# New due times for a list scheduler, and the last output tile stored in two halves

## The chip, the cores and the metric

The kernel runs on one core of one Trainium2 chip. The metric is the device time of one execution in microseconds. Three runs of the kernel before the change took 478.75, 477.60 and 477.36 us, a median of 477.6 us. One further execution was profiled: it took 473.72 us, of which the profile's span covers 472.0 us.

## What is computed

The reference is a transformer layer on 2048 tokens of 576 features: a layer norm, a segmented attention with a running memory, a residual, a second layer norm, a two-layer network with GELU, and a second residual. Cut to what matters:

```
x: [1, 2048, 576]; 32 heads of 18; 4 segments of 512 tokens; F = 4608
q, k, v = layernorm(x) @ wq, @ wk, @ wv
for each segment s:
    p     = softmax(q_s k_s^T * scale + causal mask)
    a_dot = p @ v_s
    a_mem = phi(q_s) M / (phi(q_s) z + 1e-6)       # M, z: sums over earlier segments
    o_s   = g * a_mem + (1 - g) * a_dot            # g = sigmoid(beta), one a head
    M, z += phi(k_s)^T v_s, sum of phi(k_s)
h   = x + o @ wo
out = h + gelu(layernorm(h) @ w1 + b1) @ w2 + b2
```

## The kernel before the change

The tokens are cut into 8 chunks of 256 (index c), each of two token tiles of 128 rows (index tl or qt). In this document tile t is tile 2c + tl, so tiles 0 to 15. Everything that is multiplied is bf16, and sums are f32 in PSUM.

The kernel is not written in the order in which it runs. It holds generators ("streams"), one for each kind of work, and a small planner that interleaves them while the program is being built:

- stream_P (two of them, one a tile of each chunk): load x, layer norm (lines 420 to 440), transpose to xT, the q, k, v products (lines 417 and 418, right operand wqkv), eviction by ScalarE or VectorE (lines 497 and 498), transposes of q and k to QT and KT, and phi(k).
- stream_M: the running memory (line 576) and its copies.
- stream_A: attention in visits of 16 score products (line 618), one exp over 128x2048 on ScalarE (line 624), a causal mask on GpSimd or VectorE (lines 629 and 631), 16 products with v (line 650, called PV here), the memory products (line 673), and then `finish`, which divides and adds up into o_nat (VectorE lines 686 to 694, GpSimd line 695).
- stream_B (one a tile): transpose o_nat to xT, the product with wo (lines 417 and 418, right operand wo_t), add x, layer norm, transpose to xn2T, add b2 and store the result h to a scratch tensor hd in DRAM.
- stream_F1: the products with w1 (tails of 64 rows on line 912, main part on line 925; the first chunk on lines 885 and 887), bias on eviction (VectorE 935, ScalarE 933), GELU on ScalarE (line 947). The weights w1 are loaded again for every chunk, 512 columns at a time, by one large DMA (line 838, 512 KB) and two small ones (line 841, 32 KB each). This trio is called a w1 group here.
- stream_F2: the products with w2 (line 974, 36 for each half of 288 columns), add h (line 978, from hc, which line 963 reloads from hd), store the tile (line 981).

From chunk 2 on, transposes of x (xT<-xn) and of q and k are done by DMA, from chunk 1 on those of o (xT<-o_nat) and of the second norm (xn2T). All these, and all loads and stores but one, are issued by SyncE through line 189 and its sisters. **SyncE issues in program order**: an issue that waits for its data holds back every issue behind it.

The planner (`step`, at the end of the kernel) walks a clock of its own. Each operation has a planned duration, its data dependencies, and a due time `now + slack`. When an engine is free in the planner's clock, the ready operation with the earliest due time is issued next:

```
for o in queue[e]:
    if o.ready() <= now and (best is None or (o.due, o.made) < (best.due, best.made)):
        best = o
```

The slacks are a table of some 45 numbers, `SLACK`, one a kind of operation (`t_o` the transposes of o_nat, `w1` the weight groups, `mask` the causal masks, `sum` the GpSimd sum into o_nat, and so on). Three more, `lead`, `balance` and `alone` with `linger`, choose which stream TensorE takes next. `PHASES` is a list of (time, changes): when the planner's clock passes a time, the table is updated. Before the change it has 8 entries after the initial table: at 30, 40, 100, 130, 160, 220, 320 and 360 us. The chip knows nothing of these times. All that is left of them on the chip is **the fixed order of the instructions on each engine**.

Of the kernel before, what the change touches and what calls it, by code (L numbers as in the profile page):

```python
# [16 lines left out]
def kernel(  # L17
# [15 lines left out]
    nc = tc.nc  # L33
    P = 128
    x = A_x.flatten_outer_dims()
    of = out.flatten_outer_dims()
# [4 lines left out]
    NCH = S // Q  # L41
# [17 lines left out]
    def sbuf(name, shape, dt=BF16):  # L59
        return sb.tile([P] + shape, dt, name=name)  # L60
# [9 lines left out]
    SLACK = dict(zero=19, head=36, lnp=38.5, lnb=53, pow=-202, apply=-44.5, ek_k=497.5, relu_k=102, min_k=61, add_k=34.5,  # L70
                 mz=152.5, exp=-105.5, ek=-79.5, relu=-88.5, min=192.5, add=160, hb=-200.5, gelu=56, finish=35.5, mem=-80,
                 sum=23.5, out=-77.5, hd=122.5, xp=-148, xb=-22.5, t_x=-121.5, t_q=365, t_k=36, t_o=175.5, t_h=161, w1=101,
                 w2=116.5, hc=-15, evict=-236.5, qk=-22.5, ot=126.5, mask=78.5, lead=42.5, balance=254, alone=0, linger=1.5,
                 g=9.5, x1=80, hold=-133.5, ln0=-100)
    PHASES = [(30, dict(zero=31.5, head=69.5, lnp=42, pow=-174, apply=-18.5, ek_k=572, relu_k=123, min_k=-8, add_k=97, mz=106.5,
                        exp=-54.5, ek=-116, relu=-108, min=107, add=93.5, hb=-324.5, gelu=23, mem=-91.5, sum=101, out=-68.5, hd=157,
                        xp=-263, xb=-6, t_x=-129, t_q=354.5, t_k=103, t_o=169.5, t_h=165, w1=131.5, w2=55, hc=105.5, evict=-327.5,
                        qk=-50.5, ot=42.5, mask=66, lead=41.5, balance=124, g=87.5, x1=50.5, hold=-192.5, ln0=34.5)),
              (40, dict(zero=42.5, head=90.5, lnp=70.5, lnb=54, pow=-230, apply=-8.5, ek_k=562, relu_k=120, min_k=-17.5, add_k=55.5,
                        mz=109, exp=-26.5, ek=-166.5, relu=-81, min=99.5, add=85.5, gelu=18.5, finish=19.5, mem=-67.5, sum=115,  # L80
                        out=-75.5, hd=194, xp=-259, xb=-60, t_x=-133, t_k=49.5, t_o=146, t_h=205, w1=129.5, w2=-3.5, hc=124.5,
                        evict=-359.5, qk=-86, ot=26, mask=65, lead=42.75, balance=118, linger=1, g=88.5, x1=47, hold=-202.5,
                        ln0=85.5)),
              (100, dict(zero=10.5, head=94.5, lnp=22.5, lnb=46, apply=-5.5, relu_k=153, min_k=-12.5, mz=117, exp=21.5, ek=-169,
                        min=99, add=89.5, hb=-307, gelu=26, sum=115.5, out=-60.5, xp=-288.5, xb=-55.5, t_x=-114, t_q=353.5,
                        t_k=48.5, t_o=131, t_h=216.5, w1=130, w2=-19.5, hc=124, evict=-323.5, qk=-104, ot=30, mask=53, lead=41.75,
                        balance=117.5, g=86.5, x1=31, hold=-200.5)),
              (130, dict(lnp=38, lnb=63.5, relu_k=119, min_k=-28, add_k=105, mz=66.5, min=116, add=113.5, gelu=21, finish=17,
                        mem=-95.5, sum=133, t_x=-113, t_q=352, t_o=170, w1=123.5, w2=83.5, evict=-359.5, mask=70, lead=42.25,
                        x1=66.5, hold=-184.5, ln0=35)),  # L90
              (160, dict(zero=-30, head=52, lnp=36.5, lnb=80, pow=-237, apply=-37.5, ek_k=649, relu_k=225, min_k=3, add_k=42.5,
                        mz=36, exp=-28.5, ek=0, relu=-118.5, min=95.5, add=61.5, hb=-372.5, gelu=16, finish=12.5, mem=-133.5,
                        sum=123, out=-107.5, hd=219, xp=-333.5, xb=-93, t_x=-80.5, t_q=338, t_k=89.5, t_o=196, t_h=205.5, w1=124.5,
                        w2=101, hc=197.5, evict=-388.5, qk=-68.5, ot=23.5, mask=34.5, lead=37.75, balance=116, linger=2.5, g=112,
                        x1=55.5, hold=-120.5, ln0=-55)),
              (220, dict(head=-75, lnp=4.5, lnb=77, pow=-250, apply=-3, ek_k=675, relu_k=249.5, min_k=-6, add_k=138, mz=-68, exp=-38,
                        ek=2, relu=-158, min=129.5, add=53, hb=-380, gelu=10.5, finish=-7, mem=-85, sum=125, out=-97.5, hd=166.5,
                        xp=-354.5, xb=-44, t_x=-87, t_q=371.5, t_k=169, t_o=155, t_h=225.5, w1=139, w2=105.5, hc=214.5,
                        evict=-346.5, qk=-100.5, ot=31, lead=43, balance=141, linger=1, g=138.5, x1=56.5, hold=-173, ln0=-88.5)),
              (320, dict(zero=-28, head=-73, lnb=77.5, apply=-2, relu_k=281.5, add_k=136, mz=-68.5, relu=-142, hb=-396, finish=-7.5,  # L100
                        hd=174.5, xp=-350.5, xb=-45.5, t_x=-47, t_q=371, t_k=169.5, qk=-84, ot=27, mask=74.5, alone=0.3, x1=89.5,
                        ln0=-89)),
              (360, dict(zero=-34, lnp=5.5, lnb=93.5, pow=-238, ek_k=659, relu_k=282.5, min_k=-9, mz=-118.5, exp=-35, ek=17,
                        relu=-158, min=121.5, add=51, hb=-392, finish=24.5, sum=142.5, out=-96.5, hd=167.5, xp=-354.5, xb=-6,
                        t_q=355, t_k=153.5, t_o=154, t_h=181, w1=139.5, w2=109.5, hc=233.5, evict=-376.5, qk=-83, ot=26.5,
                        mask=73.5, lead=44.75, balance=135, alone=0.6, linger=0.3, g=170, x1=75.5, hold=-175))]
    ops = []
    now, dma_free, table, tiling = 0.0, 0.0, "exp", 128
    SWITCH = 0.092
# [8 lines left out]
    class Op:  # L118
        start, end, at, apart, two, hold, ways = None, NEVER, None, False, False, 0.0, None
# [42 lines left out]
    def op(eng, dur, issue, rd=(), wr=(), slack=0.0, table=None, port=None, n=2, mode=128):  # L162
        o = Op(eng, dur, issue, preds_of(rd, wr), now + slack, table)
        o.n, o.mode = n, mode
        o.port = eng == "POOL" if port is None else port
        ops.append(o)
        queue[eng].append(o)
        note(o, rd, wr)
        return o
# [7 lines left out]
    def transfer(o, kb, first, rd, wr, receipt=0.0):  # L177
        d = Op("DMA", kb, None, (), 0.0)
        d.first, d.receipt = first, receipt
        o.moves = d  # L180
        note(d, rd, wr)
        return d

    def dma(kb, issue, rd=(), wr=(), slack=0.0):
        return transfer(op("SP", 0.5, issue, rd, wr, slack), kb, 1.6, rd, wr, {288: 0.1, 144: 0.7, 576: 0.8, 72: 0.6, 864: 1.4}.get(kb, 1.0))
# [114 lines left out]
    ek = sbuf("ek", [H, Dh])  # L300
# [6 lines left out]
    hc = sbuf("hc", [HALF], F32)  # L307
    ot = sbuf("ot", [D])
# [3 lines left out]
    hd = tc.dram_tile([S, D], F32, name="hd")  # L312
# [99 lines left out]
    def mm(n):  # L412
        return n * MM + 0.003
# [541 lines left out]
    def stream_F2():  # L955
        for c in range(NCH):
            hT = hTs[c % 2]
            for tl in range(2):
                t = 2 * c + tl
                for hf in range(2):  # L960
                    hs = slice(hf * HALF, (hf + 1) * HALF)
                    yield need(lambda: c in gelued, bank_slots, [("hT", c % 2, 0)])
                    dma(144, lambda t=t, hs=hs: nc.sync.dma_start(out=hc[:], in_=hd[t * P:(t + 1) * P, hs]), [("hd", t)], ["hc"], SLACK["hc"])
                    b = bank_slots.take()
                    for f in range(0, NF, 4):
                        hk = [("hT", c % 2, f // 2), ("hT", c % 2, f // 2 + 1)]
                        if f:
                            yield need(None, None, hk)
                        work["F2"] += 0.5

                        def go(f=f, b=b, hT=hT, tl=tl, hs=hs):
                            acc = banks[b][:, 0:HALF]
                            for q in range(f, f + 4):
                                nc.tensor.matmul(out=acc, lhsT=hT[:, q, tl * P:(tl + 1) * P], rhs=w2_sb[:, q, hs],  # L974
                                                 start=(q == 0), stop=(q == NF - 1))

                        op("PE", 4 * mm(HALF), go, hk + [("w2", f // 6), ("w2", (f + 3) // 6)], [b], n=8)
                    op("DVE", 0.45, lambda b=b, hs=hs: nc.vector.tensor_tensor(out=ot[:, hs], in0=banks[b][:, 0:HALF], in1=hc[:], op=ALU.add),
                       [b, "hc"], [("ot", hf)], slack=SLACK["ot"])
                    bank_slots.give(b)  # L980
                dma(144, lambda t=t: nc.sync.dma_start(out=of[t * P:(t + 1) * P, :], in_=ot[:]), [("ot", 0), ("ot", 1)], (), SLACK["out"])
            done_F2.add(c)

    F1, F2 = stream_F1(), stream_F2()
# [107 lines left out]
```

## Time and profile before

| what | value |
|---|---|
| median of three runs | 477.6 us (477.36 to 478.75) |
| the profiled execution, and its span | 473.72 us, 472.0 us |
| TensorE (PE) busy | 462.4 us, 98% of the span, 6102 matmuls |
| ScalarE (ACT) busy | 337.7 us, 72% |
| VectorE (DVE) busy | 272.8 us, 58% |
| GpSimd (POOL) busy | 182.6 us, 39% |
| DMA | 80.9 MB, mean 171 GB/s |
| first matmul starts, last matmul ends | 1.24 us, 468.85 us |
| granted TensorE clock | 1.0 throughout |

An engine's share is taken over the whole span. TensorE is the engine that is busy nearly all the time, so a microsecond saved on another engine shows in the time only where TensorE would have waited for it. A matmul counts as busy until its result is out, which is later than the moment at which the next one can start. The distance from one matmul's start to the next one's is therefore the better measure of what a product costs: 122 ns for 288 columns, 109 ns for 256, 182 ns for 432, 25 ns for a PV product.

### The profile page before, as it was taken

What the parts mean: (1) busy time and instruction counts of PE and PEld (TensorE: products, weight loads), DVE (VectorE), ACT (ScalarE), POOL (GpSimd) and SP (SyncE); (2) the same over time, 40 slices, a digit from 0 to 9 for tenths busy, and PEclk for the clock granted to TensorE, in tenths of its full rate; (3) what the DMA queues carried; (4) which work ended last, traced back from release to release, by engine and by line L of the source; (5) the groups of instructions that cost most, each with busy time, mean ns of one, the idle gap of its engine ahead of it and who ended that gap; (6) DMA issues with size and microseconds to landing.
All of it is one profiled execution on the core that took longest, in us unless ns stands there. A gap on an engine that the chain in (4) does not pass through costs nothing.

```text
span 472.0 us, 14508 instructions
## 1 busy us (share of the span) xinstructions
PE 462.4 (98%) x6102; PEld 350.5 (74%) x6102; DVE 272.8 (58%) x695; ACT 337.7 (72%) x331; POOL 182.6 (39%) x242
## 2 busy tenths in 40 slices
PE   8999999998999999999999999999999999999997
PEld 6768777675677777666687777677777788888875
DVE  4899975997765444788764438767545341111101
ACT  6787769966898868877678687877869787355400
POOL 4666451794734323778452306557224010000000
PEclk9999999999999999999999999999999999999999
DMA  8997878577986555979766658879565478543011
GB/s 231 269 304 236 162 159 257 105 159 153 162 231 183 143 152 171 192 146 199 111 139 195 179 168 214 149 208 232 171 184 166 132 207 238 181 134 108 26 50 50
DMA packets 123009, 80.90 MB, mean 171 GB/s; under 512 B 57520, under 2 KB 120896, under 8 KB 122944
## 3 DMA queue, kind: packets, MB, share of 16 engines
q1 hardware_dynamic: 122912, 79.98, 66.5%
q8 instruction: 47, 0.77, 0.7%
q14 instruction: 18, 0.15, 0.1%
q0 software_dynamic: 32, 0.01, 0.0%
HBM read 60.03 MB, written 7.08 MB: 142 GB/s over the span
## 4 chain that ended last, share of the span: by engine, by line
PE 82%; DMA 8%; DVE 4%; POOL 2%; ACT 1%; issue 1%; SPq 0%; POOLq 0%; ACTq 0%
PE bank L974 20%; PE bank L925 18%; PE bank L417 10%; PE late L974 7%; PE ox L650 6%; DMA xT<-o_nat 4%; PE st L618 4%; PE late L925 3%; PE bank L912 3%; PE bank L418 2%; PE bank L885 2%; DMA wqkv<-in_A_wk_dram 2%; PE ox L925 1%; POOL pt L629 1%; ACT pt L624 1%; PE ox L974 1%
## 5 line engine op out<-in xcount | busy, mean ns | idle before, releaser
L624 ACT ACTIVATE pt<-st 128x2048 bf16<-128x2048 f32 x80 | 150.2, 1877 | 43.5 <-PE st L618 40.0
L974 PEld LDWEIGHTS <-hT 128*128 128x128 bf16 x1152 | 110.2, 98 | 28.2 <-ACT hT L947 0.2
L974 PE MATMUL bank<-w_sb,hT 128*128 128x288 bf16 x864 | 121.3, 286 | 0.0
L629 POOL TENSOR_SCALAR_AFFINE_SELECT pt<-pt 128x512 bf16<-128x512 bf16 x86 | 57.2, 677 | 109.1 <-ACT pt L624 104.3
L925 PE MATMUL bank<-xn2T,w1g 128*128 128x256 bf16 x688 | 84.4, 273 | 0.0
L935 DVE TENSOR_TENSOR hT<-bank,b1T 128x512 bf16<-128x512 f32 x67 | 46.2, 690 | 59.7 <-PE bank L925 59.3
L925 PEld LDWEIGHTS <-w1g 128*128 128x128 bf16 x752 | 69.3, 97 | 12.2 <-issue 3.8
L947 ACT ACTIVATE hT<-hT 128x1536 bf16<-128x1536 bf16 (+3 forms) x24 | 66.3, 2763 | 0.5
L417 PE MATMUL bank<-wqkv,xT 128*128 128x432 bf16 (+1 forms) x268 | 57.2, 336 | 0.6 <-DMA wqkv<-in_A_wk_dram 0.6
L417 PEld LDWEIGHTS <-xT 128*128 128x128 bf16 x400 | 35.4, 97 | 24.3 <-DMA xT<-o_nat 5.3
L650 PEld LDWEIGHTS <-pt 128*128 128x128 bf16 x1280 | 41.3, 96 | 7.7 <-DVE pt L631 0.3
L933 ACT ACTIVATE hT<-bank,b1T 128x256 bf16<-128x256 f32 x86 | 36.1, 471 | 15.2 <-PE bank L925 14.9
L650 PE MATMUL ox<-v_aug,pt 128*128 128x19 bf16 x1280 | 45.6, 172 | 0.3 <-DVE pt L631 0.2
L618 PE MATMUL st<-QT,KT 32*128 32x128 bf16 x1280 | 32.3, 217 | 0.2 <-ACT pt L624 0.2
L974 PE MATMUL late<-w_sb,hT 128*128 128x288 bf16 x252 | 32.0, 286 | 0.0
L665 POOL TENSOR_TENSOR pq<-ek,pq 128x512 bf16<-128x512 bf16 x24 | 27.9, 1162 | 7.7 <-DVE ek L663 7.5
L925 PEld LDWEIGHTS <-wqkv 128*128 128x128 bf16 x288 | 27.1, 98 | 4.7 <-issue 1.5
L618 PEld LDWEIGHTS <-KT 32*128 32x128 bf16 x1280 | 18.7, 92 | 14.6 <-issue 12.3
L631 DVE TENSOR_TENSOR pt<-pt,causal 128x512 bf16<-128x512 bf16 x42 | 24.9, 599 | 7.8 <-ACT pt L624 7.8
L933 ACT ACTIVATE hT<-late,b1T 128x256 bf16<-128x256 f32 x28 | 11.8, 471 | 21.9 <-PE late L925 21.7
L695 POOL TENSOR_TENSOR o_nat<-t,t 128x288 bf16<-128x288 f32 x24 | 19.9, 829 | 14.4 <-DVE t L694 14.4
L417 PE MATMUL bank<-wo_t,xT 128*128 128x288 bf16 x124 | 20.1, 286 | 3.8 <-DMA xT<-o_nat 3.3
(136 smaller groups left out, 612.4 us busy)
## 6 DMA issues: line engine op xcount, KB each, us to landing
w1g<-in_B_w_dram SPq DMA_DIRECT2D x49, 512.0 KB, 4.0
wqkv<-in_B_w_dram SPq DMA_DIRECT2D x18, 512.0 KB, 4.1
w_sb<-in_B_w_dram SPq DMA_DIRECT2D x6, 864.0 KB, 7.7
hd<-h_t SPq DMA_DIRECT2D x16, 288.0 KB, 3.3
hc<-hd SPq DMA_DIRECT2D x32, 144.0 KB, 3.0
w1g<-in_B_w_dram SPq DMA_DIRECT2D x98, 32.0 KB, 3.3
x_b<-in_A_x_dram SPq DMA_DIRECT2D x18, 144.0 KB, 4.1
hT<-in_B_w_dram SPq DMA_DIRECT2D x5, 512.0 KB, 4.9
```

Of the source, the lines that this page charges most:

```text
L417: nc.tensor.matmul(out=out_ap, lhsT=lhsT_of(slice(0, P), k), rhs=rhs_of(slice(0, P), k), start=(k == 0), stop=False)
L618: nc.tensor.matmul(out=st4[:, i, n * P:(n + 1) * P], lhsT=KTs[(c - c % 2 + kt // 2) % 3][rows, g, (kt % 2) * P:(kt % 2 + 1) * P], rhs=QTs[ ...
L624: op("ACT", 1.88, lambda: nc.scalar.activation(out=pt[:], in_=st4[:], func=ACT.Exp, scale=scale), sk, [("pt", slot, n) for n in range(4)], ...
L629: either(("POOL", 0.64, lambda part=part: nc.gpsimd.affine_select(out=part, in_=part, pattern=[[0, 4], [1, P]], compare_op=ALU.is_ge, fill ...
L631: ("DVE", 0.42, lambda part=part: nc.vector.tensor_tensor(out=part, in0=part, in1=causal[:].unsqueeze(1).to_broadcast([P, 4, P]), op=ALU.m ...
L650: nc.tensor.matmul(out=oxv[:, 4 * (g % 4) + i, :], lhsT=pts[slot][:, i, n * P:(n + 1) * P], rhs=v_augs[(2 * s0 + kt) % 6][:, 4 * g + i, :] ...
L665: op("POOL", 1.16, lambda: nc.gpsimd.tensor_tensor(out=pq[:], in0=e_g, in1=pq[:], op=ALU.add), ["ek"], ["pq"], slack=SLACK["add"])
L925: nc.tensor.matmul(out=banks[b][:, a * Q:(a + 1) * Q], lhsT=w1_main(wt)[:, k, (2 * (h % 2) + a) * P:(2 * (h % 2) + a + 1) * P], rhs=xn2T[c ...
L933: nc.scalar.activation(out=hT[:, f + a, :], in_=banks[b][:, a * Q:(a + 1) * Q], func=ACT.Identity, bias=b1T[:, f + a:f + a + 1])
L935: either(("DVE", 0.69, lambda hT=hT, f=f, b=b: nc.vector.tensor_tensor(out=hT[:, f:f + 2, :], in0=banks[b][:].rearrange("p (a w) -> p a w" ...
L947: op("ACT", (f1 - f0) * Q * 0.00083 + 0.18, lambda hT=hT, f0=f0, f1=f1: nc.scalar.activation(out=hT[:, f0:f1, :], in_=hT[:, f0:f1, :], fun ...
L974: nc.tensor.matmul(out=acc, lhsT=hT[:, q, tl * P:(tl + 1) * P], rhs=w2_sb[:, q, hs], start=(q == 0), stop=(q == NF - 1))
```

## The change

Two edits.

**The table of due times.** `PHASES` gets seven new entries, at 45, 90, 190, 240, 290, 330 and 370 us; one number (`x1`) is dropped from the entry at 320. Nothing else in the planner is changed. Two of the new entries:

```
+              (45, dict(zero=41.5, head=42.5, lnp=69, pow=-262, apply=-9, ek_k=566, relu_k=52, min_k=-9.5, add_k=57.5, exp=-30.5,
+                        relu=-65, min=107.5, add=90, gelu=-17, finish=16.5, mem=-63.5, sum=127, hd=242, xp=-253.5, t_x=-132.5,
+                        t_q=338.5, t_h=201, w1=161.5, hc=156.5, qk=-90, ot=27, lead=41.25, balance=118.5, g=90, x1=13, hold=-201.5)),
+              (90, dict(zero=-3, head=133, lnp=103, lnb=42.5, pow=-287, apply=-65.5, ek_k=456, relu_k=25, min_k=-34, add_k=73.5,
+                        mz=-11.5, exp=-194, ek=-189.5, relu=-117, min=121, add=115.5, hb=-124.5, gelu=-30, finish=-12, mem=-153,
+                        sum=140, out=-66.5, hd=211.5, xp=-158, xb=13, t_x=-52.5, t_q=437, t_k=-83, t_o=200, t_h=290.5, w1=185.5,
+                        w2=58.5, hc=215.5, evict=-384, qk=-52.5, ot=50, mask=58, lead=41, balance=90, g=67, x1=-66, hold=-139,
+                        ln0=62)),
...
```

**The last store.** Each output tile is stored by one DMA of 144 KB once both of its halves have been added up. For tile 15 alone there are now two DMAs of 72 KB, each issued after its own half:

```
                     bank_slots.give(b)
-                dma(144, lambda t=t: nc.sync.dma_start(out=of[t * P:(t + 1) * P, :], in_=ot[:]), [("ot", 0), ("ot", 1)], (), SLACK["out"])
+                    if t == 2 * NCH - 1:
+                        dma(72, lambda t=t, hs=hs: nc.sync.dma_start(out=of[t * P:(t + 1) * P, hs], in_=ot[:, hs]), [("ot", hf)], (), SLACK["out"])
+                if t < 2 * NCH - 1:
+                    dma(144, lambda t=t: nc.sync.dma_start(out=of[t * P:(t + 1) * P, :], in_=ot[:]), [("ot", 0), ("ot", 1)], (), SLACK["out"])
```

More of the change, by code (lines that the diff above doesn't have):

```diff
@@ L95 @@
                         x1=55.5, hold=-120.5, ln0=-55)),
+              (190, dict(zero=-67.5, head=88.5, lnp=35, lnb=121, pow=-183.5, apply=-47, ek_k=663.5, relu_k=265.5, min_k=12.5,
+                        add_k=16, mz=98, exp=9.5, ek=51.5, relu=-117, min=156, add=54, hb=-336.5, gelu=70, finish=18, mem=-152,
+                        sum=135, out=-151.5, hd=142.5, xp=-337.5, xb=-96, t_x=3, t_q=318.5, t_k=67, t_o=187, t_h=148, w1=182.5,
+                        w2=67.5, hc=148, evict=-390, qk=-113.5, ot=13, mask=3, lead=37.5, balance=138.5, g=148.5, x1=95.5,
+                        hold=-204.5, ln0=-50)),
               (220, dict(head=-75, lnp=4.5, lnb=77, pow=-250, apply=-3, ek_k=675, relu_k=249.5, min_k=-6, add_k=138, mz=-68, exp=-38,
@@ L99 @@
                         evict=-346.5, qk=-100.5, ot=31, lead=43, balance=141, linger=1, g=138.5, x1=56.5, hold=-173, ln0=-88.5)),
-              (320, dict(zero=-28, head=-73, lnb=77.5, apply=-2, relu_k=281.5, add_k=136, mz=-68.5, relu=-142, hb=-396, finish=-7.5,
-                        hd=174.5, xp=-350.5, xb=-45.5, t_x=-47, t_q=371, t_k=169.5, qk=-84, ot=27, mask=74.5, alone=0.3, x1=89.5,
-                        ln0=-89)),
+              (240, dict(zero=-55, head=-105.5, lnp=36.5, lnb=91.5, pow=-253.5, apply=23, ek_k=666.5, relu_k=262, min_k=-78.5,
+                        add_k=59, mz=-61.5, exp=2.5, ek=6, relu=-109, min=204.5, add=-49.5, hb=-348, gelu=3.5, finish=3, mem=-13,
+                        sum=179, out=-151.5, hd=101.5, xp=-381.5, xb=-36.5, t_x=-116.5, t_q=343.5, t_k=282.5, t_o=180, t_h=235,
+                        w1=95.5, w2=120, hc=194.5, evict=-454, qk=-86.5, ot=26, mask=-34, lead=36, balance=190.5, linger=2.5, g=213,
+                        x1=34.5, hold=-86.5, ln0=42)),
@@ new lines @@
+              (290, dict(zero=-27.5, head=-102.5, lnp=22, lnb=89.5, pow=-245, apply=-23.5, ek_k=777.5, relu_k=282, min_k=-137,
+                        add_k=15, mz=-9, exp=61, ek=-69.5, relu=-201.5, min=81.5, add=12, hb=-381, gelu=-42.5, finish=5.5, mem=-45,
+                        sum=186.5, out=-91.5, hd=186.5, xp=-452, xb=-116, t_x=52.5, t_q=358, t_k=406.5, t_o=166, t_h=341, w1=155,
+                        w2=44.5, hc=68.5, evict=-546.5, qk=-109, ot=-35, mask=-123, lead=35, balance=214, linger=4, g=327, x1=89.5,
+                        hold=-123, ln0=21.5)),
@@ new lines @@
+              (320, dict(zero=-28, head=-73, lnb=77.5, apply=-2, relu_k=281.5, add_k=136, mz=-68.5, relu=-142, hb=-396, finish=-7.5,
+                        hd=174.5, xp=-350.5, xb=-45.5, t_x=-47, t_q=371, t_k=169.5, qk=-84, ot=27, mask=74.5, alone=0.3, ln0=-89)),
+              (330, dict(zero=-20, head=-128.5, lnp=11.5, lnb=94.5, pow=-248.5, apply=-19, ek_k=787.5, relu_k=313, min_k=-113.5,
+                        add_k=84.5, mz=-51, exp=74, ek=-71, relu=-139, min=71, add=-38.5, hb=-398.5, gelu=-87, finish=-8.5,
+                        mem=-44.5, sum=155.5, out=-124.5, hd=207.5, xp=-331.5, xb=-36.5, t_x=-24.5, t_q=422.5, t_k=139.5, t_o=142,
+                        t_h=382.5, w1=123, w2=70.5, hc=13.5, evict=-539.5, qk=-92.5, ot=95, mask=62, lead=34.5, balance=193,
+                        alone=4, linger=1, g=359, x1=94, hold=-139, ln0=-106)),
@@ L105 @@
                         t_q=355, t_k=153.5, t_o=154, t_h=181, w1=139.5, w2=109.5, hc=233.5, evict=-376.5, qk=-83, ot=26.5,
-                        mask=73.5, lead=44.75, balance=135, alone=0.6, linger=0.3, g=170, x1=75.5, hold=-175))]
+                        mask=73.5, lead=44.75, balance=135, alone=0.6, linger=0.3, g=170, x1=75.5, hold=-175)),
+              (370, dict(head=-144.5, lnp=6, lnb=93, pow=-242, mz=-79.5, relu=-149, min=117.5, add=53, mem=-52.5, sum=141.5,
+                        out=-136.5, t_x=-16.5, t_k=161.5, t_h=185, w2=110.5, hc=225.5, evict=-380.5, qk=-75, mask=71.5, lead=45,
+                        balance=143, alone=1.5, g=171, hold=-207, ln0=-104))]
     ops = []
```

## The prediction, made before the changed kernel had run

> **What bounds the kernel now.** I read the page's head first, then TensorE's waits, then the chain of waits at the longest of them, then SyncE, GpSimd and the end in order of time.
>
> ```profile
> span 472.0 us, 14508 instructions
> PE 462.4 (98%) x6102; PEld 350.5 (74%) x6102; DVE 272.8 (58%) x695; ACT 337.7 (72%) x331; POOL 182.6 (39%) x242
> ```
>
> TensorE is busy for 462.4 of 472.0 us. No product is added or taken away by the change, so all that it can move is the 9.6 us in which TensorE is idle, the ends of the run among them. TensorE's own list of waits says what these are:
>
> ```profile
> PE bank L417 <- DMA xT<-o_nat: 3.3, 4, 1.5
> PE bank L1040 <- DVE pq L374: 1.2, 1, 1.2
> PE bank L417 <- DMA wqkv<-in_A_wk_dram: 0.6, 1, 0.6
> ```
>
> The second and third belong to the first 10 us. The first is the product with wo, which waits for the DMA transpose of o_nat. From matmul start to matmul start, less the usual step of the product ahead, the stalls are longer than the idle times, since a matmul counts as busy until it has drained. By that measure the stalls over 0.06 us after 55 us are, by the trace: tile 2 0.71, tile 3 0.40, tile 4 1.68, tile 7 1.02, tile 8 0.32, tile 11 0.28 (all before the first wo product of the tile, so 4.4 us), 0.19 for a w1 group at 139 us, and 1.18 in seven short ones (0.07 to 0.36) behind VectorE or a transpose of x. That is all there is to win in the middle: 5.8 us. The largest of them in the chain, and on TensorE:
>
> ```profile
> 107.83 6.04 DMA xT<-o_nat
> 113.88 0.05 issue
> 113.92 0.66 PE bank L417 x4
> ```
>
> ```profile
> 113.92 0.66 PE L417 MATMUL bank<-wo_t,xT 128*128 128x288 bf16 x4 [1.54 <-DMA xT<-o_nat]
> ```
>
> **Why tile 4 is late.** Its last PV product ended at 96.33 us, so the transpose had over 17 us, and it was issued 11 us late. Two queues held it. GpSimd made the second half of o_nat late, behind two phi(k) operations, masks and a power:
>
> ```profile
> 98.35 0.66 POOL L555 TENSOR_SCALAR phik_pad<-qk_pad 128x576 bf16<-128x576 bf16 x1
> ...
> 102.39 0.55 POOL L435 TENSOR_TENSOR rstd_p<-rstd_p,mhalf 128x1 f32<-128x1 f32 x1
> 103.03 1.20 POOL L559 TENSOR_TENSOR phik_pad<-ek,phik_pad 128x576 bf16<-128x576 bf16 x1
> 104.18 0.86 POOL L695 TENSOR_TENSOR o_nat<-t,t 128x288 bf16<-128x288 f32 x1
> ```
>
> SyncE then had other issues ahead of it, back to back:
>
> ```profile
> 104.63 1.22 SPq L189 DMA_TRANSPOSE xT<-xn  x1
> 105.94 1.18 SPq L841 DMA_DIRECT2D w1g<-in_B_w_dram  x2
> 107.20 0.54 SPq L838 DMA_DIRECT2D w1g<-in_B_w_dram  x1
> 107.83 1.21 SPq L189 DMA_TRANSPOSE xT<-o_nat  x1
> ```
>
> **What the change moves.** Its built instruction lists hold no time, but show the order on each engine. TensorE has the same 6102 matmuls; the order is the same for the first 1405 (to 92.1 us), and it switches between full, 64-row and 32-row products 242 times, once less than before. A switch costs 0.095 us (a 288-column product steps by 218 ns ahead of one, 122 ns otherwise): **-0.1**. GELU pieces, table loads and fillers keep their numbers. Six masks go from GpSimd to VectorE (0.60 us each in the groups of the page) and four evictions from VectorE to ScalarE (0.52 us each): 3.6 and 2.1 us on engines that are 58% and 72% busy over the span, so priced at nothing beside TensorE; if that cover is gone, the visit that they sit in is late by at most one of them, and that is in the allowance below.
>
> The site that counts is each tile's way from its last PV product to its first wo product. I counted the products that TensorE has between the two in each order, each at its step (122, 109, 182, 25 ns; a block of 16 scores 0.33 us). In us, before and after: tile 3 6.8 and 6.8, tile 4 15.9 and 15.0, tile 5 7.1 and 6.2, tile 6 7.2 and 7.7, tile 7 7.7 and 7.7, tile 8 11.8 and 11.2, tile 9 9.9 and 10.3, tile 11 7.7 and 7.7, tile 13 8.8 and 11.1, tile 15 5.9 and 6.7.
>
> - **Tile 4.** On GpSimd the sum into o_nat (ready at 105.04) now stands ahead of L555, L435 and L559 (0.66 + 0.55 + 1.20), so about 102.6. On SyncE one xT<-xn and one w1 group (1.31 + 1.89, from issue to issue) go behind it: issued by 107.83 - 3.2 = 104.6. With its old 6.04 it lands at 110.7; with the median of the 14 such transposes (4.3), at 108.9. TensorE wants it at 113.92 - 1.68 - 1.42 (the order puts this product 1.42 earlier on TensorE) = 110.8. The stall goes: **-1.7** (bounds -1.7 and 0). Late next is the moved xT<-xn, issued at about 107.8; the order wants it at some 114.0, and the median of 3.5 lands at 111.3.
> - **Tile 3.** SyncE issues this transpose ahead of the two small loads of the w1 group (0.70 and 0.69 from issue to issue), so 1.4 earlier for a stall of 0.40: **-0.4**.
> - **Tile 8.** SyncE's list ahead of it is unchanged, TensorE wants it 0.94 later: **-0.3**. The w1 buffer at 139 us gets 6.4 instead of 6.0 us between its last reader and its next: **-0.2**.
> - **Tiles 7 and 11.** Distance and SyncE's list are the same: 1.02 and 0.28 stay.
> - **Tile 5.** Here the distance shrinks. Before, the transpose was issued 3.04 after the last PV product, and TensorE took it 4.0 later without a wait. Now it has 6.2 - 3.0 = 3.2. Issue to landing was 2.9 (tile 12), 3.3 (13), 4.0 (14), 4.3 (median), 6.04 (4, right behind a w1 group). Nothing heavy is issued just ahead of it now: I take 3.6, **+0.4**. Bounds: 0, and 3.4 from the slowest readiness and landing seen (3.5 for tile 9, plus 6.04, less 6.2).
> - **Other new waits.** Tighter spots appear (ten reuses of a PSUM bank within 1.0 to 1.2 us instead of three; the smallest seen before without a stall was 1.1). Between nothing and as much as the short stalls of today, 1.2: **+0.5**, nearer to the low end because the shortest reuse hardly shrinks. The opposite, that the short stalls vanish, gives -1.2.
> - **The last store.**
>
> ```profile
> 468.89 0.46 DVE L978 TENSOR_TENSOR ot<-ox,hc 128x288 bf16<-128x288 f32 x1 [3.95 <-PE ox L974]
> 469.37 0.34 SPq L981 DMA_DIRECT2D out_dram<-ot  x1
> ```
>
> Its packets run from 470.21 to 470.75, and it has landed by 471.12. Half the bytes are half of 0.54: **-0.2** (bounds 0 and -0.5). The other half and its issue of 0.34 lie under the last 4.4 us of products; behind that issue waits only the load of hc, which landed at 467.06, 1.8 us before VectorE used it.
>
> Sum: -0.1 - 1.7 - 0.4 - 0.3 - 0.2 + 0.4 + 0.5 - 0.2 = **-2.0**, so 471.7 for a profiled execution of 473.72. The timed runs lie 3.9 above that one for a reason that no view shows; I take the same 2.0 from their median: **475.6**.
>
> [...]
>
> **The rivals.**
>
> 1. *The waits come back elsewhere* (0.23). For it: the order is new in most stretches from 92 to 430 us, and I have priced only the transposes and the w1 ring. The new short waits then cost 2.0 instead of 0.5: 477.1.
> 2. *Slower, at tile 5* (0.10). If o_nat of tile 5 is ready 3.5 after the last PV product and its transpose takes the 6.04 that tile 4's took, its stall is 3.4 instead of 0.4: +1.0, so 478.6. It decides the sign once it takes over 8.6 from PV to landing (6.2 + 0.4 + 2.0). Against it: no w1 group stands right ahead of it in SyncE's order.
> 3. *The timed runs stall more than the profiled one* (0.14). If their 3.9 are the same waits grown, 5.8 have become 9.7, and the part that the change removes grows with them by 1.7: -3.4, 474.2.
> 4. *The halves do not shorten the end* (0.05): as forecast, without its last term, 475.8.
>
> The forecast itself has 0.48. **Chances.** Some 0.3%, or 1.4 us, is what a measurement of this kernel can tell from no change, so faster is under 476.2 and slower over 479.0. Forecast and rival 4 spread over about 1.2 on either side (the allowance, tiles 5 and 4): two thirds of 0.53 are faster; all of rival 3 is; a quarter of rival 1: 0.55. Slower: nearly half of rival 2 and a little of rival 1: 0.07. The rest, 0.38, is within. The range runs from 473.6 (rival 3 with half a microsecond more) to 478.3 (most of rival 2 left out).
>
> **What would show it.** Right: the wait before tile 4's wo product is gone, tile 7 still waits about 1 us for its transpose, tile 5 waits under 1 us, TensorE's idle time is some 2 us less, and the last store lands 1.5 us after its issue begins. Wrong: a new line in TensorE's waits over 1 us, above all behind VectorE or a PSUM bank; tile 4 still late, which would mean that the data and not the queues held it; or a median that does not follow the profile.

## The result, and the profile after

The changed kernel took 473.12 us (median of four runs, 472.85 to 473.24), the kernel before 478.1 us (four runs, 477.36 to 478.75): **a ratio of 0.9896, 95% interval 0.9877 to 0.9914, 5.0 us faster**. I had forecast 475.6 with a range of 473.6 to 478.3: the direction was right, the size less than half. Executions more than 1.5% longer than the fastest of the same kernel are left out of all medians, ranges and ratios below, but not of the 25.2 and 17.1 in the last expectation.

The two profiled executions hardly differ: spans of 472.0 and 471.5 us. The head of the changed kernel's page, and TensorE's own list of waits (waiter, what it waited for, us in total, times, longest):

```profile
span 471.5 us, 14509 instructions
PE 463.0 (98%) x6102; PEld 350.8 (74%) x6102; DVE 270.6 (57%) x697; ACT 339.4 (72%) x335; POOL 179.1 (38%) x236
```

```profile
PE bank L447 <- DMA xT<-o_nat: 1.9, 4, 0.7
PE bank L1073 <- DVE pq L404: 1.2, 1, 1.2
PE bank L447 <- DMA xT<-xn: 0.9, 1, 0.9
PE bank L447 <- DVE r L717: 0.3, 1, 0.3
PE bank L447 <- DVE t L710: 0.3, 1, 0.3
```

The wait for xT<-o_nat has shrunk from 3.3 to 1.9 us, and a wait for a transpose of x, 0.9 us, is new. Tile 4, the longest wait before, in the changed kernel's timelines of GpSimd, SyncE and TensorE:

```profile
102.20 0.79 POOL L725 TENSOR_TENSOR o_nat<-t,t 128x288 bf16<-128x288 f32 x1
102.95 0.67 POOL L585 TENSOR_SCALAR phik_pad<-qk_pad 128x576 bf16<-128x576 bf16 x1
```

```profile
104.58 0.57 SPq L993 DMA_DIRECT2D hc<-hd  x1
105.25 1.21 SPq L219 DMA_TRANSPOSE xT<-o_nat  x1
106.55 0.54 SPq L868 DMA_DIRECT2D w1g<-in_B_w_dram  x1
```

```profile
111.26 0.65 PE L447 MATMUL bank<-wo_t,xT 128*128 128x288 bf16 x4
```

The sum into o_nat stands ahead of phi(k) and ends at 102.99 (forecast 102.6), the transpose is issued at 105.25 (forecast 104.6), and the product starts at 111.26 (forecast 110.8) with no wait. The place that took its turn is the product of x with wqkv near 299 us, in TensorE's timeline:

```profile
297.47 1.14 PE L1004 MATMUL bank<-w_sb,hT 128*128 128x288 bf16 x8
299.47 0.91 PE L447 MATMUL bank<-wqkv,xT 128*128 128x432 bf16 x4 [0.86 <-DMA xT<-xn]
```

So the profiles account for 0.5 us of 5.0. Where the rest is was the question for the experiments.

### The profile page after: what moved, and what is told of

Its sections match the earlier page's. It is cut to its first block, busy times and chain, and to the rows that moved or that the text cites. A ratio compares the mean times of both kernels' runs of the same rounds, so it can differ in the third digit from the quotient of the medians.

```text
span 471.5 us, 14509 instructions
## 1 busy us (share of the span) xinstructions
PE 463.0 (98%) x6102; PEld 350.8 (74%) x6102; DVE 270.6 (57%) x697; ACT 339.4 (72%) x335; POOL 179.1 (38%) x236
## 4 chain that ended last, share of the span: by engine, by line
PE 82%; DMA 8%; DVE 5%; POOL 2%; ACT 2%; issue 1%; SPq 0%; ACTq 0%; POOLq 0%
PE bank L1004 21%; PE bank L955 18%; PE bank L447 10%; PE ox L680 6%; DMA xT<-o_nat 5%; PE late L1004 5%; PE st L648 5%; PE bank L942 3%; PE late L955 3%; PE bank L448 3%; PE bank L1073 1%; PE bank L915 1%; ACT pt L654 1%; DMA w1g<-in_B_w_dram 1%; DMA xT<-xn 1%
## 5 line engine op out<-in xcount | busy, mean ns | idle before, releaser
L1004 PE MATMUL bank<-w_sb,hT 128*128 128x288 bf16 x936 | 129.1, 286 | 0.0
L659 POOL TENSOR_SCALAR_AFFINE_SELECT pt<-pt 128x512 bf16<-128x512 bf16 x80 | 53.0, 673 | 95.6 <-ACT pt L654 85.6
L955 PEld LDWEIGHTS <-w1g 128*128 128x128 bf16 x768 | 70.9, 97 | 13.0 <-issue 4.0
L965 DVE TENSOR_TENSOR hT<-bank,b1T 128x512 bf16<-128x512 f32 x63 | 43.4, 690 | 44.8 <-PE bank L955 44.3
L963 ACT ACTIVATE hT<-bank,b1T 128x256 bf16<-128x256 f32 x92 | 38.5, 470 | 21.0 <-PE bank L955 20.5
L661 DVE TENSOR_TENSOR pt<-pt,causal 128x512 bf16<-128x512 bf16 x48 | 27.3, 575 | 6.9 <-ACT pt L654 6.7
L648 PEld LDWEIGHTS <-KT 32*128 32x128 bf16 x1280 | 18.7, 92 | 14.2 <-issue 11.8
L955 PEld LDWEIGHTS <-wqkv 128*128 128x128 bf16 x272 | 25.8, 98 | 4.1 <-issue 0.8
L1008 DVE TENSOR_TENSOR ot<-bank,hc 128x288 bf16<-128x288 f32 x26 | 11.8, 454 | 29.3 <-PE bank L1004 23.6
L827 POOL TENSOR_TENSOR h_t<-h_t,b_bc 128x576 f32<-128x576 f32 x16 | 20.4, 1277 | 11.6 <-DVE xn L469 10.4
L963 ACT ACTIVATE hT<-late,b1T 128x256 bf16<-128x256 f32 x24 | 10.1, 470 | 19.6 <-PE late L955 19.4
```

The lines of the kernel that those rows point to most:

```text
L648: nc.tensor.matmul(out=st4[:, i, n * P:(n + 1) * P], lhsT=KTs[(c - c % 2 + kt // 2) % 3][rows, g, (kt % 2) * P:(kt % 2 + 1) * P], rhs=QTs[ ...
L659: either(("POOL", 0.64, lambda part=part: nc.gpsimd.affine_select(out=part, in_=part, pattern=[[0, 4], [1, P]], compare_op=ALU.is_ge, fill ...
L661: ("DVE", 0.42, lambda part=part: nc.vector.tensor_tensor(out=part, in0=part, in1=causal[:].unsqueeze(1).to_broadcast([P, 4, P]), op=ALU.m ...
L955: nc.tensor.matmul(out=banks[b][:, a * Q:(a + 1) * Q], lhsT=w1_main(wt)[:, k, (2 * (h % 2) + a) * P:(2 * (h % 2) + a + 1) * P], rhs=xn2T[c ...
L963: nc.scalar.activation(out=hT[:, f + a, :], in_=banks[b][:, a * Q:(a + 1) * Q], func=ACT.Identity, bias=b1T[:, f + a:f + a + 1])
L965: either(("DVE", 0.69, lambda hT=hT, f=f, b=b: nc.vector.tensor_tensor(out=hT[:, f:f + 2, :], in0=banks[b][:].rearrange("p (a w) -> p a w" ...
```

## The experiments

One property of the change made clean cuts possible. Built with only some of the new entries of `PHASES`, the order falls into two independent parts: the entries at 45 and 90 us change it up to TensorE's matmul 2819 (near 190 us) and not behind, those from 190 us on change it only behind. Ratios are to the kernel before, run beside it on the same chip, with 95% intervals.

### The kernel before again, and each part alone

`e1_before` is the kernel before, unedited. `e2_tail` has the second hunk of the diff alone. `e4_early` has the entries 45 and 90 alone, `e5_late` the entries 190, 240, 290, 330 and 370 and the edit at 320 alone:

```
 PHASES = [(30, ...), (40, ...),
+          (45, ...), (90, ...),                                        # e4_early
           (100, ...), (130, ...), (160, ...),
+          (190, ...), (240, ...), (290, ...), (330, ...), (370, ...),  # e5_late, in their places
           (220, ...), (320, ...), (360, ...)]
```

> The kernel before, unchanged, run again beside itself, with a profile. Open is why its timed median (478.1) lies 4.4 us above its one profiled execution (473.72), while the changed kernel's four runs (472.85 to 473.24) include its profiled one. Theory A (some executions of the old order lose about 4.4 us at waits that the profiled one did not have): times mostly near 478, and if the new profile falls in such an execution, its span is near 476.4, TensorE's stalls after 55 us sum to about 10 instead of 5.8, and one or a few sites carry the difference. Theory B (the profiled execution ran on a chip or at a time at which every kernel is 4 us faster): the runs here agree among themselves to 1 us and the profile shows the same 5.8 us of stalls at whatever time they have. The ratio to itself is 1.000 by either.

> The kernel before with the last tile stored in two halves, and nothing else: every engine's order is that of before but for SyncE's last two stores. My prediction's term: -0.2 us (ratio 0.9996), last store landing 1.5 us after its issue begins instead of 1.75. Rival (fixed cost of a transfer): 0.0. Both: ratio 0.999 to 1.001.

> Only the new due times at 45 and 90 us: every engine's order is that of the changed kernel up to TensorE's matmul 2819 (near 190 us) and that of before after it. Theory A1 (the extra waits of the timed runs sit in the stretch from 79 to 190 us: tiles 3 and 4, the w1 ring near 139 us): ratio 0.990 to 0.993, nearly the whole gain. Theory A2 (they sit after 190 us): ratio 0.996 to 1.000. Theory B (no extra waits, only those of the two profiles): the stalls between 79 and 190 us sum to 2.4 us in the old profile and 1.5 in the new, so -0.9 us, ratio 0.998.

> Only the new due times from 190 us on: every engine's order is that of before up to matmul 2819 (near 190 us) and that of the changed kernel after it, the last store whole. Theory A1: ratio 0.997 to 1.001. Theory A2: 0.990 to 0.993. Theory B: stalls after 190 us are 2.4 us in the old profile and 3.3 in the new one, so +0.9 us, ratio 1.002. If the two parts share the gain, e4 and e5 lie near 0.995 each and add up.

| kernel | median us | ratio | interval |
|---|---|---|---|
| before, 34 runs | 474.60 (472.97 to 478.18) | | |
| e1_before | 475.0 | 1.0011 | 0.9988 to 1.0035 |
| e2_tail | 474.99 | 0.9993 | 0.9970 to 1.0016 |
| e4_early | 472.48 | 0.9955 | 0.9932 to 0.9978 |
| e5_late | 475.6 | 1.0027 | 1.0005 to 1.0050 |

Two things follow. On this chip the kernel before runs at 474.6 and not at 478, and it spreads over 5 us; my base of three runs was not its time everywhere. And the early part carries the gain: theory A1 in kind, though -2.1 us where it asked for nearly all of 5. The late part alone costs 1.3 us, near theory B's +0.9.

**The last store** brings nothing measurable, and the trace says why. From the last matmul's end to the end of the span it is 3.17 us before, and 3.18 with the halves, alone or in the changed kernel. The store does land earlier: 1.59 us after its issue begins instead of 1.75. But at the program's end SyncE goes through six waits on DMA semaphores one after the other. Before, the last store's semaphore was the sixth, released 2.28 us after the last matmul, and all others were done. With one more DMA it is the third, released 2.13 after, and three more waits of some 0.06 us each follow it.

### The changed kernel again, and both under slow transfers

`e3_due` is the first hunk of the diff alone, `e6_after` the changed kernel. `d1_before` and `d2_after` are the two kernels with 30 foreign copies:

```
         for o in sorted(ops, key=lambda o: (o.start, o.made)):
             o.issue()
+            if o.eng == "ACT" and o.start > 20.0 + 14.0 * n_far and o.start < 440.0:
+                r = n_far % 9
+                nc.scalar.dma_start(out=far[n_far * 64:(n_far + 1) * 64, :], in_=B_w1[r * 64:(r + 1) * 64, :])
+                n_far += 1
```

> The changed due times alone, the last tile stored whole: the order of every engine is the changed kernel's but for the last stores. If the parts add up as they did alone (early -0.45%, late +0.27%): ratio to before 0.998, about -0.9 us. If the order as a whole does what the first comparison of the two kernels showed: 0.990, -5 us. Against the changed kernel itself: +0.2 us by my term for the last store, 0.0 by the fixed cost of a transfer.

> The changed kernel again, beside before on the same chip. Theory C (the first comparison, 0.9896, holds some 3 to 4 us that are no property of the two orders: four runs of before from the upper end of its spread, on a chip or at a time that was not the one of the changed kernel's runs): ratio 0.997 to 0.999, from the early part's -2.1 us and the late part's +1.3. Theory D (the old order loses more than the new where transfers are slow): near 0.998 too where before runs at 474.7, but nearer to 0.990 if before runs at 478 here, and the slow runs of before have more spread than those of the changed kernel.

> The kernel before with disturbed transfers: 30 copies of 576 KB from DRAM to DRAM that nobody reads, issued by ScalarE one every 14 us of the planner's time, all other orders unchanged. [...] Both theories: slower than before, by 2 to 12 us. It counts against the same disturbance of the changed kernel.

> The changed kernel with the same 30 copies. Theory D: it loses at least 3 us less than the kernel before does under the same copies, so the two stand at 0.990 or below to each other. Theory C: both lose the same within 1.5 us, and the ratio of the two stays at 0.996 to 1.000.

These kernels ran on another chip, and there the kernel before has a median of 477.4 us (473.68 to 480.38, 17 runs). `e3_due` took 473.74 (0.9925, 0.9899 to 0.9952) and `e6_after` 473.95 (0.9922, 0.9886 to 0.9958): -3.6 and -3.7 us by the ratios. Under the copies the kernel before took 501.31 us (four runs, 499.96 to 503.96; 1.0492, interval 1.0436 to 1.0548) and the changed one 493.03 (three runs, 488.39 to 493.76; 1.0284, 1.0216 to 1.0353): 8.3 us apart. Over its own undisturbed time the old order lost 23.9 us and the new one 19.1. **This part of theory D holds: the old order loses more than the new where transfers are made slow** (in `d1_before`'s profile, of an execution of 509.66 us, the large loads of w1 land 5.0 us after their issue in the median and xT<-o_nat 5.2, in the first profile 4.0 and 4.3). The first comparison's 478.1 is like this chip's 477.4 and not like the other's 474.6. That transfers are slower on this chip the traces bear out, as far as one execution each can: of the 344 DMAs that SyncE issues, those of `e6_after` take on the mean 0.17 us longer from issue to landing than those of `e8_after`, the same kernel on the first chip (4.07 and 3.90 us over all DMAs; 229 of the 344 are longer). Theory C in its band, 0.997 to 0.999, is out; but part of the first 5.0 us was not found again.

### Tile 4 alone, the early part on top, and one more profile

`e7_early_tail` is the early entries with the store in halves, `e8_after` the changed kernel, `e10_before` the kernel before. `e9_tile4` moves two instructions of the kernel before, picked by their place in the loops, and nothing else:

```
             if (c, qt, gh) == (2, 0, 1):
+                sooner.append(o)               # the sum into o_nat, line 695
...
                 if (c, tl) == (2, 0):
+                    sooner.append(...)         # the transpose of o_nat, line 189
...
+    for o in sooner:                           # right behind what each reads or overwrites
+        o.start = max(p.start for p in o.preds if p.start is not None) + 1e-4
```

> The early due times (45 and 90 us) and the store in halves, without the due times from 190 us on. If the late due times cost as they did by themselves (+0.27%): 1 to 2 us faster than the changed kernel, ratio to before 0.995 on a chip where before runs at 475, 0.988 where it runs at 478. If the late due times win back there what they lose (they keep the wait at 209 us, lengthen the tile 15 distance): the same as the changed kernel within 0.5 us.

> The changed kernel, on the same chip as the early part, the single move and before in one call. Theory D (the gain grows with the slowness of the transfers, which differs by chip): 0.992 where before runs at 478, 0.997 to 0.999 where it runs at 475. Theory E (the gain is 0.992 on every chip, and the sum of the parts misleads): 0.992 at either.

> The kernel before with two instructions moved and nothing else: on GpSimd the sum that completes tile 4's o_nat goes ahead of two phi(k) operations and the powers, and on SyncE the transpose of tile 4's o_nat goes ahead of the issues that the old order has before it. TensorE, VectorE and ScalarE keep their order. My step for tile 4 (-1.7 us, seen as 1.0 to 1.7 in four profiles of the old order): ratio 0.996 to 0.998, and the wait of TensorE at 112 us is gone. If it only moves the wait to the transposes of x behind it: 0.999 to 1.001. If a long wait also slows TensorE's clock for some us after it, the gain is more than the wait, up to 3 us, and runs with a mean clock of 0.996 become rarer.

> The kernel before, for one more profile on the chip of these runs. Where it runs at 478, TensorE's waits before wo and w1 products should sum to 3 to 4 us more than in the first profile (5.8 after 55 us), spread over the sites before 190 us that the changed kernel relaxes (tiles 3 and 4, the w1 groups at 135 and 139 us) if theory A1 holds, or over all of them evenly if the transfers are just slower everywhere.

On the first chip again (kernel before 475.09, 35 runs): `e7_early_tail` 472.36 (0.9946, 0.9924 to 0.9968), `e8_after` 472.7 (0.9941, 0.9914 to 0.9967), `e9_tile4` 475.32 (1.0008, 0.9982 to 1.0034), `e10_before` 474.35 (0.9994, 0.9965 to 1.0023). So the changed kernel is 2.4 us faster on this chip by the medians and 2.8 by the ratio. `e8_after` was also to tell theory D from theory E, a gain of 0.992 on every chip. D's band for a chip like this, 0.997 to 0.999, is missed; E's 0.992 lies inside the interval and is not excluded. So the undisturbed runs do not show that the gain depends on the chip. On this chip the early part alone does as well as the whole; the cost that the late part had alone does not show on top of the early part, and I do not know why. No other version is clearly faster than the changed kernel.

Tile 4's move gained nothing. TensorE's list of waits in `e9_tile4`:

```profile
PE bank L418 <- DMA xT<-o_nat: 2.2, 5, 0.6
PE bank L418 <- DMA xT<-xn: 1.3, 1, 1.3
```

The long wait for o_nat is gone (longest 0.6), and a wait of 1.3 us for the transpose of x stands at 109 us in its place: moved ahead of `hc` and a w1 group, the o_nat transpose had pushed xT<-xn from 104.63 (first profile) to 106.58. That is the second of the two answers in the expectation. The new profile of the kernel before showed another wait, which the first one has at 0.19 us. TensorE's timeline of `e10_before`:

```profile
139.85 0.28 PE L912 MATMUL bank<-xn2T,w1g 64*128 64x256 bf16 x1 [0.37 <-DMA w1g<-in_B_w_dram]
140.88 0.39 PE L912 MATMUL bank<-xn2T,w1g 64*128 64x256 bf16 x3 [0.75 <-DMA w1g<-in_B_w_dram]
```

Together 1.36 us from start to start, for the weights of the next group. No profile of the early part's order (`after`, `e3_due`, `e4_early`, `e6_after`, `e7_early_tail`, `e8_after`) has a wait there. The extra that theory A1 looked for (3 to 4 us of stalls) is not in this profile, whose time of 473.89 is one of the faster ones.

### Taking single waits away

`f1_tile3` has the entry at 45 us alone. `f5_tile4b` moves tile 4's sum as in `e9_tile4`, but its transpose only ahead of the w1 group right before it, behind xT<-xn. `f3_later4` was to put it two issues later. `f4_no_w1` and `g1_no_w1` leave out the loads of two w1 groups; their products then take what the buffers hold.

```
+    moved["sum"].start = max(p.start for p in moved["sum"].preds) + 1e-4    # f5_tile4b
+    moved["t"].start = sp[at - 4].start + 1e-4                              # f5_tile4b
+    moved["t"].start = sp[at + 2].start + 1e-4                              # f3_later4
...
+        skip = n in (16, 17)                                                # g1_no_w1: (14, 15)
+        dma(512, lambda: skip or nc.sync.dma_start(out=w1_main(wt), ...
```

> The entry at 45 us alone. Every engine's order is that of before, but for three of SyncE's issues: the transpose of tile 3's o_nat goes ahead of the two small w1 loads. My step for tile 3: -0.4 us, ratio 0.999, the wait at 84 us (0.3 to 1.1 us in the profiles of before) gone. Rival: the transpose waits for DMA time and not for its issue, since the profiles of the changed kernel have 0 to 1.0 us there: 1.000, the wait stays.

> The kernel before with one issue of SyncE moved: the transpose of tile 4's o_nat goes behind the transpose of x and the load of x_b that the old order has after it, so it is issued about 1.9 us later. TensorE's wait at 112 us, 1.0 to 1.7 before, becomes 2.9 to 3.6. If only waiting counts: +1.9 us, ratio 1.004. If a wait of about 3 us also lowers TensorE's granted clock for some us behind it: mean clock 0.996 or less in most runs, matmul steps doubled behind the wait, and +3.5 us or more, ratio 1.007 to 1.009.

> The kernel before without the loads of two w1 groups (the last two of chunk 1, used near 135 and 139 us); the products there take what the buffers hold, so the output differs. Nothing waits for them. If these waits (0.2 to 1.4 us in the profiles of before, 0 in those of the changed kernel) are what the typical execution loses: -0.8 to -1.4 us, ratio 0.997 to 0.998, and the free DMA time helps tile 6 besides. If they are covered by what follows: 1.000.

> The kernel before with two instructions moved: GpSimd's sum for tile 4 ahead of the phi(k) operations and powers, as in e9_tile4, but SyncE's transpose of tile 4's o_nat only ahead of the w1 group right before it, behind the transpose of x that it displaced in e9_tile4. It is issued some 1.9 us earlier. My step for tile 4: -1.0 to -1.7 us, ratio 0.9965 to 0.998, no wait over 0.3 us at 108 to 113 us, and fewer runs with a mean clock of 0.996. If the wait comes back at the w1 group that now stands behind it: 0.999 to 1.000.

> The kernel before without the loads of the two w1 groups that TensorE waits for at 135 and 139 us (their products take what the buffers hold, so the output differs). The waits there, 0.3 to 1.4 us together in the old order's profiles, go. If they count in full: -0.5 to -1.3 us, ratio 0.997 to 0.999. If the time comes back at the next wait (tile 6, tile 7): 0.999 to 1.000.

| kernel | median us, before | ratio | interval |
|---|---|---|---|
| f1_tile3 | 474.9, 475.11 | 1.0007 | 0.9990 to 1.0023 |
| f3_later4 | 473.5, 475.11 | 0.9974 | 0.9955 to 0.9993 |
| f4_no_w1 | 475.25, 475.11 | 1.0008 | 0.9984 to 1.0032 |
| f5_tile4b | 473.37, 475.11 | 0.9971 | 0.9951 to 0.9992 |
| g1_no_w1 | 473.82, 474.7 | 0.9969 | 0.9944 to 0.9995 |

- **Tile 3** (`f1_tile3`): no gain, and the wait is there as before, 0.47 us. The rival was right that it is not its issue that the transpose waits for: it was issued at 79.43 instead of 80.79 us (first profile) and landed at 84.91 instead of 84.74. That DMA time is what it waits for is my estimate, from the DMA share of 0.99 that the first profile has from 80 to 84 us.
- **Tile 4** (`f5_tile4b`): -1.4 us by the ratio, no wait at 112 us or at the transpose of x. `f3_later4` agrees by accident: two issues later is behind the wo product in the program, so that product no longer waits for the transpose and takes what the buffer held. It measures the wait taken away, -1.2 us, and not the wait made longer, which was therefore not tried.
- **The w1 groups**: `f4_no_w1` left out groups used at 143 and 147 us, where nothing waits, and its profile still has 0.8 us of waits at 134 to 139; two loads (1.1 MB) less gained nothing. `g1_no_w1` left out the right ones: its profile has no wait there, and the time falls by 1.5 us by the ratio. TensorE's timeline at the place:

```profile
137.73 1.51 PE L975 MATMUL bank<-w_sb,hT 128*128 128x288 bf16 x11
139.18 0.39 PE L913 MATMUL bank<-xn2T,w1g 64*128 64x256 bf16 x4
```

**The clock.** The profiled execution of `f5_tile4b` took 476.57 us, with a mean granted clock of 0.996. The table of stretches shows what such a run is (stretch, length, then busy time with instructions in brackets of TensorE, its weight loads, VectorE, ScalarE and GpSimd; granted clock, DMA share, GB/s):

```profile
80.00:84.00 4.00, 4.00 (x36) 3.01 (x36) 2.94 (x8) 3.97 (x4) 0.49 (x1) 1.00 1.52 290
84.00:87.00 3.00, 0.95 (x9) 0.68 (x8) 1.45 (x6) 2.97 (x3) 1.46 (x4) 1.00 0.54 123
87.00:90.50 3.50, 3.50 (x29) 1.78 (x28) 2.55 (x8) 3.48 (x2) 2.05 (x5) 0.52 0.27 36
90.50:95.00 4.50, 4.50 (x47) 3.00 (x46) 3.05 (x9) 3.33 (x3) 2.88 (x4) 0.99 0.65 66
```

```profile
86.17 0.66 PE L418 MATMUL bank<-wo_t,xT 128*128 128x288 bf16 x4 [2.05 <-DMA xT<-o_nat]
```

TensorE waited 2.05 us for tile 3's transpose in this execution; the DMA share from 80 to 84 us is 1.52, and 0.99 in the first profile. Behind the wait the granted clock is 0.52 in the 3.5 us from 87.0 to 90.5: TensorE's steps are 0.12 to 0.18 us longer there, so the wait cost about another 1.7 us, an estimate (0.48 of these 3.5). Of all 183 runs with the old early order (`before`, `e1`, `e2`, `e5`, `e10`), 33 have a mean clock of 0.996 or less; of 60 with the new one (`after`, `e3`, `e4`, `e6`, `e7`, `e8`), one. Such a run of the kernel before is longer by 1.8 to 2.4 us on the first two chips (medians 476.5 to 474.1 and 476.8 to 474.7 on the first, 478.6 to 476.8 on the second), and by 0.9 and 2.3 on two more, where there were only two and three of them. At 18% of the runs 1.8 to 2.4 us are 0.3 to 0.4 us in the mean. Which wait starts it in the kernel before is not shown, since no such run of it was profiled without the copies: `f3_later4`'s profile has the low clock in its second slice (11.8 to 23.7 us, between 0.8 and 0.9), with a wait of 2.1 us for wqkv at a place where both orders are the same, and the wait of tile 3 is in the changed kernel too. So why the new order has such runs so seldom stays open.

### Which part bears the slow transfers

`g2_d_early` has the 30 copies on `e7_early_tail`.

> The early due times and the store in halves, with the 30 foreign copies of d1_before and d2_after. On one chip the old order lost 25.2 us under them and the changed kernel stood 17.1 above the undisturbed kernel before. If the early part carries the tolerance: 14 to 19 us above the undisturbed kernel before, ratio 1.030 to 1.040. If the late due times do: 22 to 26 above, ratio 1.046 to 1.055.

495.43 us beside 474.7 (1.0434, 1.0392 to 1.0475), on one more chip: +20.7, between the +23.9 of the old order and the +15.6 of the whole change, both taken from the undisturbed kernel before, and between the two bands that I had set. By these differences the early part bears 3.2 of the 8.3 us. By the times themselves (501.31 for the old order, 495.43, and 493.03 for the whole change) it bears 5.9. Since the kernels ran on different chips, with 2.7 us between their times of the kernel before, this stays open.

## Why the prediction was wrong

By its own steps:

- **TensorE's work unchanged, -0.1 for a switch.** Both profiles are 98% busy with 6102 matmuls; a tenth of a microsecond is less than any run here can tell.
- **Tile 4, -1.7.** Right: -1.4 by `f5_tile4b` (interval -2.3 to -0.4). The late-next check was right as well, and needed: without the changed order's later product with wqkv, the gain moves into the transpose of x, as `e9_tile4` shows.
- **Tile 3, -0.4.** Wrong: no gain was measured (`f1_tile3`, interval -0.5 to +1.1), and the wait stayed. The changed kernel's profiles still have 0.89 (`after`) and 0.21 us (`e8_after`) there; the issue was not what it waited for.
- **The w1 buffer, -0.2.** Mis-sized: I took the 0.19 of one execution as the price of a margin. In five profiles with the old early order (`before`, `e1`, `e2`, `e5`, `e10`) this place waits 0.2, 0, 1.0, 1.0 and 1.4 us, 0.7 in the mean, and taking it away gains 1.5 (interval 0.2 to 2.7).
- **Tile 8, -0.3; tiles 7 and 11 as before.** Tile 8 kept 0.47 us. Tile 7 went from 1.02 to 0.48 and tile 11 from 0.28 to 0.57, with no change of order around them. That is within what such a wait varies by: in the same five profiles tile 7's is from under 0.15 to 1.02 us.
- **Tile 5, +0.4.** Its transpose landed 3.27 us after issue (I took 3.6), and there was no wait in the profile, 0.25 at most in `e6_after`. The place is tight all the same: under the copies TensorE waits 3.7 us for this transpose in `g2_d_early`'s profile.
- **Other new waits, +0.5.** Too low: the transpose of x near 299 us alone costs 0.7 to 1.15 in the profiles of the late part's order, and 0.44 at 93 us comes with the early part. I had placed the risk in PSUM reuse; it came from a transpose that I had counted as safe by its distance.
- **The last store, -0.2.** 0.0, as rival 4 had it, but not because the halves land no earlier: the store did land 0.16 us earlier (1.59 us after its issue begins instead of 1.75), near the 0.2 that I had taken from its packets, and the waits behind it in SyncE's list gave it back.
- **"I take the same 2.0 from their median."** This is the step that failed, and with it the size of the w1 term above. I priced each wait from one execution of 473.72 us and took the sum unchanged to timed runs of 477.6; measured was -5.0. Run beside the kernel before again, the change is worth 2.8 us where that one runs at 475 (1.6 to 4.1, by the ratio) and 3.7 where it runs at 477.4 (2.0 to 5.4). The waits are not a constant: the w1 groups, counted at 0.2, are worth 1.5, and under the copies the old order lost 23.9 us and the new one 19.1. The profiled execution looks like one of the first chip: its DMAs take 3.87 us in the mean from issue to landing, those of the kernel before on the first chip 3.90 and 3.91. The timed runs look like the second chip. So the 3.9 us between them were the sign of a slower base, and I let them stand as a constant. How much the gain grows on the slower chip is not shown: by the means it is 3.4 us there (`e3_due` and `e6_after` together) and 2.4 on the first (`e8_after`), 1.0 apart with a standard error of 0.6. Rival 3, which let the waits grow (474.2), came nearest, at a chance of 0.14.
- **That the sum of -2.0 is near the -2.4 to -2.8 of the first chip is in part luck.** The w1 term was 1.3 us too small, against 0.4 for tile 3, 0.2 for the store and too little for the new waits on the other side; the clock was not in the sum at all.

What stays open: on the chip where the kernel before runs at 477.4 I have no profile of it without the copies, so which of its waits grow there in the plain run is not shown; and why the first comparison's 0.9896 lies below all repeats (0.9922 and 0.9941).

## What to carry to other kernels

A wait in one profile is one draw. Where an engine is 98% busy, price the margins that an order leaves to its transfers, and take several executions on more than one chip before trusting a base. If the timed runs lie above the profiled one by more than their spread, give weight to the case that they come from a slower chip or are themselves waits, and that what a change removes grows with them. When a transfer is moved ahead in SyncE's order, what it passes can become late (in `e9_tile4` xT<-xn went from 104.63 to 106.58 us, and TensorE waited 1.3 us for it): the gain is real only if the consumer of that has also moved.

## What the runs showed of the hardware

- A TensorE wait of about 2 us cost more than itself. In `f5_tile4b` 2.05 us idle before 86.17 us were followed by 3.5 us (87.0 to 90.5) at a granted clock of 0.52, by the estimate above another 1.7 us. `f3_later4` has a wait of 2.1 us for wqkv and a clock between 0.8 and 0.9 in the slice from 11.8 to 23.7 us. In `before` the longest wait was 1.54 us, and the clock 1.00 in every stretch of 30 us.
- The same program differs by 2.8 us between chips (474.6 and 477.4, medians of 34 and 17 runs), and not by the granted clock alone: the second chip's runs with a mean clock above 0.996 have a median of 476.8, against 474.1. The same 344 DMAs took 0.17 us longer each in the mean there (`e6_after` beside `e8_after`, one profile of each chip).
- An earlier landing of the last store did not end the program earlier: in `after` it came 1.59 us after its issue began, in `before` 1.75, but three further semaphore waits behind its own took 0.19 us, and from the last matmul to the end it is 3.18 and 3.17 us.
